# Linear attention with a routed expert layer on one core: the projection of the queries moved behind the first half of the products with the queries

## The chip, the core and the metric

The kernel runs on one core of a Trainium2 chip. The metric is the device time in microseconds (us) of one execution, the median of several runs. TensorE (PE in the profile; PEld is its loading of weights) does the matmuls, VectorE (DVE) and ScalarE (ACT) read their results out of PSUM, GpSimd (POOL) works in SBUF only, and SyncE (SP) issues most transfers.

## What is computed

The reference is a linear attention, whose rows then go through an expert layer that picks one expert per row. The change lies in the attention:

```python
def phi(x):
    proj = np.einsum('bhsd,df->bhsf', x, w_phi)
    proj = proj - np.max(np.abs(proj), axis=-1, keepdims=True)
    return np.concatenate([np.exp(proj), np.exp(-proj)], axis=-1)
q_p, k_p = (phi(q), phi(k))
kv = np.einsum('bhsf,bhsd->bhfd', k_p, v)
z = np.sum(k_p, axis=2)
num = np.einsum('bhsf,bhfd->bhsd', q_p, kv)
den = np.einsum('bhsf,bhf->bhs', q_p, z)[..., None] + 1e-06
return (num / den).astype(np.float32)
```

There are 8 batches, 8 heads, 576 rows of 64 numbers each, and 128 features; everything is float32. After it come 4608 rows of 512 for 8 experts (512 to 1024 and back).

## The kernel before

The attention is cut into 16 units (one batch, four heads) and each unit into two pairs of heads, so there are 32 steps for the keys and 32 for the queries. A software pipeline runs over iterations t = 0 to 37 (line 836). Each iteration works on a different stage of several steps at once: the keys' step t is transposed, that of t-1 projected, that of t-2 exponentiated and summed; the queries run two steps behind the keys (`lag`), and are projected at t-3, turned and exponentiated at t-4, and multiplied with the sums at t-5.

What an iteration does, in which order, is a string of letters in the table `CFG` (line 22): `order` has one string for even t and one for odd t, and `ends` has strings of its own for t = 34, 35 and 36. From t = 3 on the engines take the instructions in just that order (`man`: PE, DVE, ACT and POOL are scheduled by hand). The letters that matter here are these.

- `v` (`st_turn_more`, lines 441 to 465, even t only): transposes on PE into the PSUM tile `ps_V`, of the sums over keys (`kvs`) and of the queries' last rows (`ut`). ACT empties the tile by one copy to `kvt` (line 453) and two exponentials to `eqt` (line 462).
- `0`, `1`, `2` (`st_proj`, lines 386 to 409): projections on PE into a PSUM tile `ps_A` of two banks, `1` of a key step, `2` of a query step, `0` of the last rows (odd t only). There are two such tiles (`nb`, A: 2). DVE reads each twice (lines 405 and 406) and writes `u`.
- `a`, `b`, `c`, `d`: these two DVE instructions for `0` (a), `1` (b) and `2` (d); `c` holds the reciprocals and the transposes of the inputs.
- `K`: the two exponentials of a key step on ACT (line 420).
- `Q` (`st_turn_q`, lines 430 to 439): sixteen transposes of the queries' `u` on PE, into the same PSUM tag `ps_V`, of which there is one buffer (line 423). `e` and `E` are the two exponentials that ACT makes of them (line 437).
- `u` and `w` (`st_use_q`, lines 532 to 562): the first and the second half of the products of the queries with the sums, into `ps_O`, each emptied by ACT (line 549).
- `x` and `z` (`st_use_k`, lines 469 to 490): the sums over keys of the first and the second head, into `ps_K` (line 476).
- `l` (`st_logits`) and `y` (`st_use_qt`): small products behind them. `B` takes a bank of `ps_K`. `L`, `P`, `R`, `r` run what was put off: the routing of finished batches.

The loop that reads the strings is short:

```python
for c in CFG["ends"].get(t, CFG["order"][t % 2]):
    ...
    elif c == "2":
        x = pair("q", t - F - 1)
        if x:
            mx["2"] = st_proj([x[0]], x[1])
    ...
    elif c in "uw":
        if uq:
            st_use_q(*uq, int(c == "w"))
```

Of the kernel before, what the change touches and what calls it, by code (L numbers as in the profile page):

```python
# [18 lines left out]

P = 128  # L20
SLOT = 256
CFG = {'late': 1, 'sp': 1, 'gp': (6, 8, 11, 14, 16, 19, 21), 'rows': 9.0, 'tab': (2, 2, 3, 4, 5, 6, 7, 8, 9, 10, 11, 12, 15, 19, 31), 'ql': 0, 'cp': 0, 'seq': ('E', 'E', 'E', 'C', 'C', 'SC', 'C', 'DS', 'C', 'D'), 'post': (4, 8, 6), 'post2': (3, 5, 5), 'pk': (0, 2, 4), 'man': (3, 38), 'eng': ('PE', 'DVE', 'Activation', 'Pool'), 'nb': {'K': 1, 'O': 1, 'A': 2, 'P': 3, 'U': 2}, 'apools': (('ld', 2), ('hl', 4), ('up', 5), ('zp', 2), ('ep', 7), ('kvp', 5), ('ac', 1), ('xp', 3)), 'mpools': (('wseta', 1), ('mx', 1), ('mo', 2), ('wsetb', 1), ('wsetc', 1), ('rawq', 1)), 'lag': (2, 2, 3, 0), 'order': ('LPv12KQebRcdBuExzwlr', 'LP01aKQ2ebRcdBuExwzyr'), 'vl': 0, 'at': 1, 'eb': (2, 2), 'ub': 4, 'stage': (2, 2, 4, 4), 'stage2': (1, 2, 3, 3), 'dve': ('0', '1', 'ntkq', '2', 'n2', 'tkq', 'n2t'), 'pd': 1, 'vq': 0, 'qq': 1, 'xb': 4, 'whole': 'k', 'vb': 1, 'af': 1, 'wg': 2, 'q0': 1, 'out6': 2, 'ends': {34: '2dcvQeuEFBwlLRPr', 35: 'QcueERwyLXPr', 36: 'cuwRyLPr'}}


@with_exitstack
def kernel(
# [51 lines left out]
    edge.tile([P, 56], F32, name="edge")  # L78
    for nm, bufs in CFG["apools"]:
        c, side = (lctx, "right") if nm in ("ld", "hl") else (actx, "left")  # L80
        pools[nm] = c.enter_context(tc.tile_pool(name=nm, bufs=bufs, side=side))
    ac = pools["ac"]
    NB = CFG["nb"]

# [200 lines left out]
    with actx:  # L285
# [44 lines left out]
        def st_load(u, eng=nc.sync, more=None):  # L330
            whole = u.kind in CFG["whole"]
            w = D if whole else 32
            whole = whole and u.g >= CFG["wg"]
            u.raw = ld.tile([P, 2, 18, w], F32, tag="raw" + u.kind, name="raw", bufs=2)
            for pr in range(1 if whole else 2):
                for hd in range(2):
                    for dh in range(2):
                        r = slice((2 * hd + dh) * 32, (2 * hd + dh) * 32 + 32)
                        src = kv_in[u.kind][u.g][hd * 32:hd * 32 + 32]
                        if whole:  # L340

                            n = 18 * D - 32
                            nc.sync.dma_start(
                                out=u.raw[r].rearrange("p r t c -> p r (t c)")[:, :, 0:n],
                                in_=src[:, :, dh * 32:dh * 32 + n])
                        else:
                            (more if more and pr == 1 else eng).dma_start(
                                out=u.raw[r, pr, :, 0:32],
                                in_=src[:, pr].rearrange("p (t c) -> p t c", c=D)[:, :, dh * 32:dh * 32 + 32])

        def st_loadv(u):
            u.v0 = ld.tile([P, 4, 4 * D], F32, tag="v", name="v", bufs=CFG["vb"])
            u.vt = vts[u.g % len(vts)]
            for q4 in range(4):
                nc.sync.dma_start(
                    out=u.v0[q4 * 32:q4 * 32 + 32].rearrange("p h (t c) -> p h t c", c=D),
                    in_=vv[u.g][:, :, 4 * q4:4 * q4 + 4, :],
                )

            u.v1 = ld.tile([32, 4, 2 * D], F32, tag="v1", name="v1", bufs=CFG["vb"])  # L360
            nc.sync.dma_start(
                out=u.v1, in_=vv[u.g][:, :, 16:18, :].rearrange("p h t c -> p h (t c)"))
# [1089 lines left out]
```

## Time and profile before

| | us |
|---|---|
| median of 3 runs | 581.87 |
| lowest and highest | 579.68, 582.03 |
| the profiled execution's own time | 578.38 |
| its span, first to last instruction | 576.2 |
| the attention's pipeline, about t = 4 to t = 33 | 25.3 to 297 of the span |
| PE busy in that stretch | 250.22 of 271.70 |

A row of the timeline gives the start, the time from the first start to the last end of a run of like instructions, engine, line, what is written and read, the count, and in brackets the idle time ahead of it with what ended it. The records of one projection are 16, of `Q` 16, of `u` or `w` 32. Matmuls are pipelined, so how long a block holds up PE is read from its start to the next block's start, not from its duration.

### The profile page before, as it was taken

To read this page: it belongs to the slowest core of one execution; us is meant where nothing else is said; L and a number is where in the kernel's file an instruction comes from. 1 tells how busy PE (TensorE), PEld (TensorE's weight loads), DVE (VectorE), ACT (ScalarE), POOL (GpSimd) and SP (SyncE) were. 2 spreads that over 40 slices of the span, in tenths; PEclk is the share of its full clock that TensorE was granted. 3 is DMA by queue.
4 is the path that set the end of the run, shared out by engine and by line. 5 is a ranking of instruction groups with operands and counts; after the bars stand their busy time and mean duration, and the time that the engine had idled before them with its cause. 6 is when DMAs were issued, how large, how long until landed. Compare 5 with 4: busy or idle time off the path is not lost. (4 is left out here: it accounts for less than half of the span.)

```text
span 576.2 us, 20682 instructions
## 1 busy us (share of the span) xinstructions
PE 522.2 (91%) x8606; PEld 485.4 (84%) x8606; DVE 447.4 (78%) x790; ACT 341.9 (59%) x606; POOL 282.7 (49%) x520
## 2 busy tenths in 40 slices
PE   2888999998999898998989999799999989999993
PEld 2788999888998888998988898699889878988892
DVE  3887788988778887797966897778879898868840
ACT  1457676677666776677665443745676757646620
POOL 4213335635547354564546256683749571558011
PEclk9989999999999999999999999899999999999998
DMA  7878878788987989875367895679577986867400
GB/s 147 176 166 163 168 160 211 194 170 174 243 205 194 195 174 224 201 183 122 130 211 270 251 335 179 180 247 335 167 254 241 325 289 233 276 205 250 171 20 32
DMA packets 151233, 116.25 MB, mean 202 GB/s; under 512 B 91875, under 2 KB 126819, under 8 KB 150114
## 3 DMA queue, kind: packets, MB, share of 16 engines
q1 hardware_dynamic: 140704, 104.51, 66.7%
q0 software_dynamic: 3200, 9.45, 4.6%
q10 hardware_dynamic: 7234, 0.95, 1.0%
q8 instruction: 69, 1.13, 0.8%
q14 instruction: 26, 0.21, 0.1%
HBM read 91.66 MB, written 24.02 MB: 201 GB/s over the span
## 5 line engine op out<-in xcount | busy, mean ns | idle before, releaser
L217 POOL TENSOR_TENSOR w<-wraw_c,w 128x256 fp32r<-128x256 f32 x84 | 81.1, 994 | 54.2 <-ACT w L212 38.4
L405 DVE TENSOR_REDUCE m<-ps_A 128x8 f32<-128x1024 f32 x64 | 77.0, 1203 | 35.7 <-PE ps_A L395 35.7
L217 DVE TENSOR_TENSOR w<-wraw_c,w 128x1024 fp32r<-128x1024 f32 x71 | 94.0, 1340 | 12.8 <-ACT w L212 12.5
L212 ACT ACTIVATE w<-wraw_c 128x1024 fp32r<-128x1024 f32 x92 | 93.8, 1050 | 7.4 <-DMA wraw_c<-in_moe_w_dram 7.4
L476 PE MATMUL ps_K<-vm,ek 128*64 128x65 f32 x2048 | 79.9, 224 | 5.4 <-issue 3.0
L406 DVE TENSOR_TENSOR u<-ps_A,m 128x1024 f32<-128x1024 f32 x64 | 78.3, 1224 | 3.9
L545 PE MATMUL ps_O<-kva,eq 128*64 128x74 f32 x1984 | 76.8, 229 | 4.6 <-issue 4.0
L395 PE MATMUL ps_A<-wsrc,xT 64*128 64x128 f32 x1024 | 73.1, 289 | 7.2 <-DVE u L406 4.5
L476 PEld LDWEIGHTS ps_K<-vm,ek 128*64 128x64 f32 x2048 | 73.0, 140 | 5.5 <-issue 4.7
L545 PEld LDWEIGHTS ps_O<-kva,eq 128*64 128x64 f32 x1984 | 68.8, 136 | 8.2 <-issue 4.6
L395 PEld LDWEIGHTS ps_A<-wsrc,xT 64*128 64x128 f32 x1024 | 65.8, 199 | 10.2 <-DVE u L406 4.8
L437 ACT ACTIVATE eq<-ps_V 128x1024 f32<-128x1024 f32 x64 | 65.7, 1030 | 9.6 <-PE ps_V L428 9.6
L420 ACT ACTIVATE ek<-u 128x1024 f32<-128x1024 f32 x64 | 64.1, 1057 | 2.3 <-DVE u L406 2.3
L1110 PE MATMUL ps_O<-w,hh 128*128 128x512 f32 x160 | 63.7, 398 | 0.0
L1029 POOL DMA_INDIRECT out_dram<-o,si x22 | 28.8, 1307 | 59.5 <-DVE si L1025 46.0
L549 ACT ACTIVATE os<-ps_O 128x296 f32<-128x296 f32 x62 | 26.1, 420 | 48.4 <-PE ps_O L545 46.4
L1115 PE MATMUL ps_O<-w,hlo 128*128 128x512 f32 x120 | 47.2, 394 | 0.0
L1114 PE MATMUL ps_O<-w,hh 128*128 128x512 f32 x120 | 47.0, 391 | 0.0
L524 POOL TENSOR_TENSOR xm<-os,rec 128x512 f32<-128x512 f32 x32 | 33.4, 1045 | 24.9 <-DVE rec L523 21.5
L384 DVE STREAM_TRANSPOSE xT<-raw 128x512 f32<-128x512 f32 x64 | 40.5, 669 | 1.2 <-DMA raw<-in_k_dram 1.2
L476 PE MATMUL ps_K<-vt,ekt 128*64 128x65 f32 x512 | 37.7, 224 | 0.0
L1110 PEld LDWEIGHTS ps_O<-w,hh 128*128 128x128 f32 x160 | 30.1, 188 | 6.1
(283 smaller groups left out, 1084.9 us busy)
## 6 DMA issues: line engine op xcount, KB each, us to landing
wraw_c<-in_moe_w_dram SPq DMA_DIRECT2D x96, 512.0 KB, 5.3
raw<-in_k_dram SPq DMA_DIRECT2D x56, 280.0 KB, 5.3
raw<-in_q_dram SPq DMA_DIRECT2D x120, 72.0 KB, 4.6
xrows<-xm SPq DMA_DIRECT2D x8, 1028.0 KB, 5.8
v<-in_v_dram SPq DMA_DIRECT2D x64, 128.0 KB, 3.4
out_dram<-xm SPq DMA_DIRECT2D x32, 256.0 KB, 4.8
xrows<-xt SPq DMA_DIRECT2D x4, 257.0 KB, 6.0
v<-in_v_dram SPq DMA_DIRECT2D x16, 64.0 KB, 3.1
```

The costliest lines, as they stand in the source:

```text
L212: nc.scalar.activation(out=hi, in_=raw, func=AF.Copy)
L217: eng.tensor_tensor(out=lo[:, r], in0=raw[:, r], in1=hi[:, r].bitcast(F32), op=ALU.subtract)
L395: nc.tensor.matmul(p[:, hd, j * NF:(j + 1) * NF], xT[r], wsrc[r], start=True, stop=True)
L405: lambda: nc.vector.tensor_reduce(out=m, in_=pv, axis=AX.X, op=ALU.max, apply_absolute_value=True),
L406: lambda: nc.vector.tensor_tensor(out=uu, in0=pv, in1=m.rearrange("p h (j o) -> p h j o", o=1).broadcast_to([P, 2, n, NF]), op=ALU.subtract),
L420: nc.scalar.activation(out=o, in_=uu, func=AF.Exp, scale=(1.0, -1.0)[a])
L437: return [lambda a=a: nc.scalar.activation(out=e[:, a].rearrange("p s g c -> p s (g c)"), in_=t, func=AF.Exp, scale=(1.0, -1.0)[a]) for a ...
L476: nc.tensor.matmul(o[s * 64:s * 64 + 64, hd, half, :], e[:, half, s * 64:s * 64 + 64], x, start=(g == 0), stop=(g == 4))
L545: q_last[0] = nc.tensor.matmul(ov[s * 64:s * 64 + 64, 2 * j + hd, :], e[:, half, s, 4 * hd + 2 * th + j], kva[:, half, 2 * pr + hd, :], st ...
L1110: nc.tensor.matmul(y[sub], hh[:, t], wh[:, fi, :], start=first, stop=False)
L1114: nc.tensor.matmul(y[sub], hh[:, t], wl[:, fi, :], start=False, stop=False)
L1115: nc.tensor.matmul(y[sub], hlo[:, t], wh[:, fi, :], start=False, stop=last)
```

## The change

Two strings of `order` change, one for even and one for odd t:

```diff
-'order': ('LPv12KQebRcdBuExzwlr', 'LP01aKQ2ebRcdBuExwzyr')
+'order': ('LPv1KQeub2RcBdExzwlr', 'LP01aKQeu2bRcBdExwzyr')
```

On even t the queries' projection `2` goes from its place behind that of the keys, `1`, to one behind the products `u`; on odd t it goes from behind `Q` to behind `u`. To make that so, `u` is moved ahead of the DVE's chains `b`, `c`, `d`. The strings for t = 34 to 36 stay.

PE, an even iteration (t = 6). Before: `kvs` and `ut` are the transposes `v`, `xT_931` belongs to the keys and `xT_932` to the queries, `u_984` or `u_1004` is read by `Q`, `ps_O` is `u`, and `ps_K` is `x`.

```order
L428 MATMUL ps_V_1104<-ident_101,kvs_894 128x64 x8
L428 MATMUL ps_V_1104<-ident_101,ut_939 128x64 x4
L395 MATMUL ps_A_1122<-wsrc_114,xT_931 128x128 x8
L395 MATMUL ps_A_1133<-wsrc_114,xT_932 128x128 x8
L428 MATMUL ps_V_1150<-ident_101,u_984 128x64 x16
L545 MATMUL ps_O_1182<-kva_565,eq_957 64x74 x16
L476 MATMUL ps_K_1180<-vm1_110,ek_1147 64x65 x8
```

The same place now:

```order
L428 MATMUL ps_V_1104<-ident_101,kvs_894 128x64 x8
L428 MATMUL ps_V_1104<-ident_101,ut_939 128x64 x4
L395 MATMUL ps_A_1122<-wsrc_114,xT_931 128x128 x8
L428 MATMUL ps_V_1139<-ident_101,u_1004 128x64 x16
L545 MATMUL ps_O_1159<-kva_565,eq_957 64x74 x16
L395 MATMUL ps_A_1179<-wsrc_114,xT_932 128x128 x8
L476 MATMUL ps_K_1197<-vm1_110,ek_1136 64x65 x8
```

Between the transposes into `ps_V` of `v` and those of `Q`, which reuse the one buffer, there stands one projection, where two stood; the other now stands between two blocks of products.

PE, an odd iteration (t = 7), before: `xTt` is `0`, `xT_1086` the keys' projection `1`, `xT_1093` the queries' `2`.

```order
L395 MATMUL ps_A_1282<-wsrc_114,xTt_1094 128x128 x2
L395 MATMUL ps_A_1289<-wsrc_114,xT_1086 128x128 x8
L428 MATMUL ps_V_1305<-ident_101,u_1143 128x64 x16
L395 MATMUL ps_A_1323<-wsrc_114,xT_1093 128x128 x8
L545 MATMUL ps_O_1346<-kva_892,eq_1151 64x74 x16
L476 MATMUL ps_K_1344<-vm1_110,ek_1302 64x65 x8
```

And now:

```order
L395 MATMUL ps_A_1282<-wsrc_114,xTt_1094 128x128 x2
L395 MATMUL ps_A_1289<-wsrc_114,xT_1086 128x128 x8
L428 MATMUL ps_V_1305<-ident_101,u_1189 128x64 x16
L545 MATMUL ps_O_1325<-kva_892,eq_1140 64x74 x16
L395 MATMUL ps_A_1343<-wsrc_114,xT_1093 128x128 x8
L476 MATMUL ps_K_1361<-vm1_110,ek_1302 64x65 x8
```

Here `2` and `u` have changed places. DVE, POOL and SP keep their order throughout. On ACT the emptying of `u` (line 549) moves ahead of two small instructions of the routing (lines 647 and 660) where an iteration has one.

More of the change, by code (lines that the diff above doesn't have):

```diff
@@ L21 @@
 SLOT = 256
-CFG = {'late': 1, 'sp': 1, 'gp': (6, 8, 11, 14, 16, 19, 21), 'rows': 9.0, 'tab': (2, 2, 3, 4, 5, 6, 7, 8, 9, 10, 11, 12, 15, 19, 31), 'ql': 0, 'cp': 0, 'seq': ('E', 'E', 'E', 'C', 'C', 'SC', 'C', 'DS', 'C', 'D'), 'post': (4, 8, 6), 'post2': (3, 5, 5), 'pk': (0, 2, 4), 'man': (3, 38), 'eng': ('PE', 'DVE', 'Activation', 'Pool'), 'nb': {'K': 1, 'O': 1, 'A': 2, 'P': 3, 'U': 2}, 'apools': (('ld', 2), ('hl', 4), ('up', 5), ('zp', 2), ('ep', 7), ('kvp', 5), ('ac', 1), ('xp', 3)), 'mpools': (('wseta', 1), ('mx', 1), ('mo', 2), ('wsetb', 1), ('wsetc', 1), ('rawq', 1)), 'lag': (2, 2, 3, 0), 'order': ('LPv12KQebRcdBuExzwlr', 'LP01aKQ2ebRcdBuExwzyr'), 'vl': 0, 'at': 1, 'eb': (2, 2), 'ub': 4, 'stage': (2, 2, 4, 4), 'stage2': (1, 2, 3, 3), 'dve': ('0', '1', 'ntkq', '2', 'n2', 'tkq', 'n2t'), 'pd': 1, 'vq': 0, 'qq': 1, 'xb': 4, 'whole': 'k', 'vb': 1, 'af': 1, 'wg': 2, 'q0': 1, 'out6': 2, 'ends': {34: '2dcvQeuEFBwlLRPr', 35: 'QcueERwyLXPr', 36: 'cuwRyLPr'}}
+CFG = {'late': 1, 'sp': 1, 'gp': (6, 8, 11, 14, 16, 19, 21), 'rows': 9.0, 'tab': (2, 2, 3, 4, 5, 6, 7, 8, 9, 10, 11, 12, 15, 19, 31), 'ql': 0, 'cp': 0, 'seq': ('E', 'E', 'E', 'C', 'C', 'SC', 'C', 'DS', 'C', 'D'), 'post': (4, 8, 6), 'post2': (3, 5, 5), 'pk': (0, 2, 4), 'man': (3, 38), 'eng': ('PE', 'DVE', 'Activation', 'Pool'), 'nb': {'K': 1, 'O': 1, 'A': 2, 'P': 3, 'U': 2}, 'apools': (('ld', 2), ('hl', 4), ('up', 5), ('zp', 2), ('ep', 7), ('kvp', 5), ('ac', 1), ('xp', 3)), 'mpools': (('wseta', 1), ('mx', 1), ('mo', 2), ('wsetb', 1), ('wsetc', 1), ('rawq', 1)), 'lag': (2, 2, 3, 0), 'order': ('LPv1KQeub2RcBdExzwlr', 'LP01aKQeu2bRcBdExwzyr'), 'vl': 0, 'at': 1, 'eb': (2, 2), 'ub': 4, 'stage': (2, 2, 4, 4), 'stage2': (1, 2, 3, 3), 'dve': ('0', '1', 'ntkq', '2', 'n2', 'tkq', 'n2t'), 'pd': 1, 'vq': 0, 'qq': 1, 'xb': 4, 'whole': 'k', 'vb': 1, 'af': 1, 'wg': 2, 'q0': 1, 'out6': 2, 'ends': {34: '2dcvQeuEFBwlLRPr', 35: 'QcueERwyLXPr', 36: 'cuwRyLPr'}}
 @with_exitstack
```

## The prediction

> **What bounds the kernel now.** The page comes first: which engine is full, and for how long.
>
> ```profile
> span 576.2 us, 20682 instructions
> ...
> PE 522.2 (91%) x8606; PEld 485.4 (84%) x8606; DVE 447.4 (78%) x790; ACT 341.9 (59%) x606; POOL 282.7 (49%) x520
> ```
>
> PE leads over the whole span. The change touches only the attention's pipeline, so the second view is the table of stretches for it, whose columns are the length of the stretch and each engine's busy time in it.
>
> ```profile
> 25.30:297.00 271.70, 250.22 (x6543) 240.71 (x6541) 224.47 (x393) 183.81 (x333) 127.23 (x296) 0.99 0.78 180
> ```
>
> PE is busy for 250.22 of 271.70 us there, at a granted clock of 0.99; DVE follows with 224.47. So an instruction's worth of time added to PE is lost, unless PE would have idled for it. Where PE idles now is in the waits of PE in this same stretch (engine and line, what it waited for, us in total, times, longest).
>
> ```profile
> PE ps_A L395 <- DVE u L406: 4.5, 5, 1.3
> PE ps_O L545 <- issue: 4.0, 3, 1.8
> PE ps_K L476 <- issue: 3.0, 4, 1.1
> ...
> PE ps_A L395 <- DVE ut L406: 1.1, 5, 0.2
> ```
>
> Two of these waits belong to projections: PE waits for DVE to hand back a `ps_A` tile, five times for 0.9 us in the mean, at `1` of an odd iteration, and five times shortly at `2` of an odd iteration. The rows with "issue" are seven idle stretches that nothing in the profile ends. These rows are what may hide a new delay.
>
> **The part on even iterations: `Q` loses its cover.** The timeline of PE in an even iteration (t = 18) shows the order in which the one `ps_V` buffer is used twice.
>
> ```profile
> 150.74 0.47 PE L428 MATMUL ps_V<-ident,kvs 64*128 64x64 f32 x8
> 151.04 0.29 PE L428 MATMUL ps_V<-ident,ut 64*128 64x64 f32 x4
> 151.16 2.01 PE L395 MATMUL ps_A<-wsrc,xT 64*128 64x128 f32 x32
> 153.00 0.67 PE L428 MATMUL ps_V<-ident,u 64*128 64x64 f32 x16
> 153.60 1.25 PE L545 MATMUL ps_O<-kva,eq 128*64 128x74 f32 x32
> 154.68 0.64 PE L476 MATMUL ps_K<-vm,ek 128*64 128x65 f32 x16
> ```
>
> The 32 records at 151.16 are `1` and `2`; behind them `Q` starts at 153.00 without a wait. ACT in the same iteration:
>
> ```profile
> 151.86 0.66 ACT L462 ACTIVATE eqt<-ps_V 128x256 f32<-128x256 f32 x2
> ...
> 153.00 2.01 ACT L420 ACTIVATE ek<-u 128x1024 f32<-128x1024 f32 x2
> 154.90 1.03 ACT L437 ACTIVATE eq<-ps_V 128x1024 f32<-128x1024 f32 x1
> ```
>
> `Q` may not write `ps_V` before `eqt` is read out, at 151.86 + 0.66 = 152.52, which is 1.78 us behind the start of `v`. There is a place in the trace where nothing stands between: t = 34, whose own string has `v` and `Q` side by side.
>
> ```profile
> 297.37 0.41 PE L428 MATMUL ps_V<-ident,kvs 64*128 64x64 f32 x8
> ...
> 299.14 0.58 PEld L428 LDWEIGHTS ps_V<-ident,u 64*128 64x128 f32 x16 [1.38 <-ACT eqt L462]
> ```
>
> There `Q` starts 1.77 us behind `v` and has waited for `eqt`. With `1` alone between them, PE would be ready for `Q` one projection after 151.16. How long a projection holds PE ahead of `Q` is in the next odd iteration (t = 19):
>
> ```profile
> 160.12 1.06 PE L395 MATMUL ps_A<-wsrc,xT 64*128 64x128 f32 x16
> 161.02 0.66 PE L428 MATMUL ps_V<-ident,u 64*128 64x64 f32 x16
> 161.90 1.16 PE L395 MATMUL ps_A<-wsrc,xT 64*128 64x128 f32 x16 [0.22 <-DVE ut L406]
> 163.00 1.19 PE L545 MATMUL ps_O<-kva,eq 128*64 128x74 f32 x30
> ```
>
> It is 161.02 - 160.12 = 0.90, so PE is ready at 152.06, and waits until 150.74 + 1.77 = 152.51: a new stall of 0.45 us in each even iteration, of which there are fifteen (t = 4 to 32).
>
> **The part on both kinds: two more changes of shape.** The rows also say how the weights lie: `64*128` for `v`, `0`, `1`, `2` and `Q`, `128*64` for `u`, `w`, `x`, `z` and `l`. Before, an iteration has all of the first shape together; now `2` stands between `u` and `x`, and PE goes to the second shape, back, and there again. Blocks that meet at such a border are further apart. From an odd iteration (t = 17):
>
> ```profile
> 140.62 0.72 PE L395 MATMUL ps_A<-wsrc,xTt 64*128 64x128 f32 x8
> 142.30 1.16 PE L395 MATMUL ps_A<-wsrc,xT 64*128 64x128 f32 x16 [0.96 <-DVE u L406]
> 143.29 0.66 PE L428 MATMUL ps_V<-ident,u 64*128 64x64 f32 x16
> 143.78 1.11 PE L395 MATMUL ps_A<-wsrc,xT 64*128 64x128 f32 x16
> 144.83 1.25 PE L545 MATMUL ps_O<-kva,eq 128*64 128x74 f32 x32
> ...
> 145.91 0.63 PE L476 MATMUL ps_K<-vm,ek 128*64 128x65 f32 x16
> ```
>
> A projection ahead of products takes 144.83 - 143.78 = 1.05, against the 0.90 ahead of `Q`. `Q` ahead of a projection takes 0.49, ahead of products (153.00 to 153.60) 0.60. For products ahead of a projection, which the pipeline does not have now, the nearest rows are the 32 records of `y` ahead of one (t = 33), and for a projection ahead of sums those of t = 3:
>
> ```profile
> 295.24 1.20 PE L589 MATMUL ps_O<-kva,eqt 128*64 128x74 f32 x32
> 296.37 0.83 PE L395 MATMUL ps_A<-wsrc,xT 64*128 64x128 f32 x10
> ```
>
> ```profile
> 21.75 1.16 PE L395 MATMUL ps_A<-wsrc,xT 64*128 64x128 f32 x16 [0.72 <-DVE ut L406]
> 22.84 0.69 PE L476 MATMUL ps_K<-vm,ek 128*64 128x65 f32 x16
> ```
>
> 1.13 and 1.09; for the latter I take 1.05, as ahead of products, since t = 3 lies in the start. Now the two iterations can be laid out. Even, from `v` to `x`: before 154.68 - 150.74 = 3.94. After: `Q` at 1.77, then 0.60, 1.13 and 1.05, so `x` at 4.55: 0.61 more, 0.45 of it the stall and 0.16 the borders. Odd, from `Q` to `x`: before 145.91 - 143.29 = 2.62; after 0.60 + 1.13 + 1.05 = 2.78: 0.16 more. Per pair 0.77, over fifteen pairs 11.55 us, if nothing hides it.
>
> **What hides it.** First, the five long waits of PE for `u` at `1` of an odd iteration. DVE's row there starts from `1` of the even iteration, which doesn't move, and the wait ends when DVE is done; a PE that comes 0.61 later waits 0.61 less. 5 x 0.61 = 3.05 (the waits have 0.9 each). Second, the wait at `2` of an odd iteration goes: at t = 19 it stands 0.88 behind `Q` (161.02 to 161.90), at t = 17 0.49, so 0.39 each, and behind `u` the tile is long free. 5 x 0.39 = 1.95; by the idle times of the row alone, 1.1. Left are 11.55 - 3.05 - 1.95 = 6.55. Third, the idle stretches with "issue". Six of the seven stand in an even iteration behind `Q`, the first and the last of the four at line 476 being
>
> ```profile
> 122.23 0.22 PE L476 MATMUL ps_K<-vm,ek 128*64 128x65 f32 x1 [1.06 <-issue]
> ...
> 248.33 0.57 PE L476 MATMUL ps_K<-vm,ek 128*64 128x65 f32 x13 [0.52 <-issue]
> ```
>
> and none of the six is ahead of a long wait. If what ends them comes at a time of its own, each swallows up to 0.61: 6 x 0.61 = 3.66, and 2.89 are left. The Trainium skill, "Runtime: NRT & Kernel Launch", section "Instruction fetch mechanics", says that crossing from one block of fetched instructions to the next is mostly hidden; by that there would be no such idle time, nothing to swallow, and 6.55 would be the sum. The trace disagrees: the two rows of waits hold 7.0 us. So the sum lies between 2.9 and 6.55. I take 4.1, nearer to the lower end, because short waits at `1` that end under the modelled tail of `0` are not in the row and cover some too.
>
> What else moves costs nothing. DVE takes the result of `2` later than PE gives it:
>
> ```profile
> 157.51 1.19 DVE L405 TENSOR_REDUCE m<-ps_A 128x8 f32<-128x1024 f32 x1
> ...
> 165.60 1.19 DVE L405 TENSOR_REDUCE m<-ps_A 128x8 f32<-128x1024 f32 x1
> ```
>
> Even, `2` starts at 150.74 + 3.50 = 154.24 and is done 1.16 later, at 155.4, DVE comes at 157.51: 2.1 to spare. Odd, it starts at 161.02 + 0.61 + 1.73 = 163.36 and is done at 164.5, DVE comes at 165.60: 1.1 to spare. ACT's first exponential of `Q` waits for `ek` until 154.90, while `Q` is done at about 153.2. On ACT the emptying of `u` goes ahead of two small instructions; at worst they shift by one such copy and nobody on PE waits for them. SP's queue is the same, so no transfer moves by order.
>
> **The sum.** On the profiled execution 578.38 + 4.1 = 582.5. That run is 3.5 below the median of 581.87, with no row that says why, so the change is put on the median: 586.0. About 0.5% (2.9 us) is what a measurement of this kernel can tell from no change: slower means above 584.8, faster below 579.0.
>
> **The rivals.**
>
> *Covered after all (not slower).* The distance between blocks of different shape could be a matter of the buffers they touch and not come twice; then only the stalls count: 15 x 0.45 = 6.75, less 5 x 0.45 for the long waits, 1.95 at the odd `2`, and 6 x 0.45 = 2.7 in the issue stretches: -0.15. Time 581.7. It decides if `2` behind `u` starts 1.03 and not 1.13 later and `x` 0.90 behind `2`. For it: the covers are large, and two of the border's four numbers are taken from other blocks. Against it: both border prices that the pipeline has (1.05 against 0.90, 0.60 against 0.49) point the same way.
>
> *Nothing hides it (much slower).* The issue stretches stay, the waits of DVE move along with PE, since DVE's own inputs come from PE: 581.87 + 11.55 = 593.4. The Trainium skill, "Perfetto Trace Analysis", section "Optimization Strategy", says that the same gap repeating on the engine that should be saturated can mean that PSUM lacks room for the next tile; a gap ahead of `Q` would be just that, and by this rule it is a loss in each iteration. Against it: in the five pairs with a long wait DVE starts from `1`, ahead of the stall.
>
> *The stall feeds the issue (faster).* If the seven stretches come from PE's instructions arriving late, a PE that waits 0.45 us in each even iteration may let them arrive, and the seven go: -7.0. With the stalls alone left over (6.75 - 2.25 - 1.95 = 2.55) that makes -4.5, 577.4. It decides when at least 5.5 of the 7.0 us go and the borders are free. For it: 7.0 us are there to be had. Against it: a stretch of 1.8 is not cured by 0.45.
>
> **How the numbers follow.** The forecast, 2.9 to 6.55 more (584.8 to 588.4), has 0.60; covered after all 0.25; nothing hides it 0.06; faster 0.09. The forecast is slower but for its lowest edge, 0.51 of it, and so is the second rival: 0.57. No change is 0.25 and 0.09 of the forecast: 0.34. Faster 0.09. The range leaves out the second rival and most of the third, and allows for the spread of the runs of before at both ends: 580.0 to 590.0.
>
> **What would show it.** Right: in the waits of PE a row `ps_V` L428 <- ACT `eqt` of about fifteen times, 0.3 to 0.5 each; `Q` 1.77 behind `v` on even t; the row of `ut` gone; the row of `u` at `1` cut from 4.5 to about 1.5; `x` about 1.05 behind `2`. Wrong: if the `eqt` row is missing, if DVE waits for `ps_A` at `d`, or if the issue rows change by several us, since then the sum is not what decides. The experts' stage, from 297 on, should take as long as before.

## The result, and the profile after

The changed kernel takes 584.45 us (median of 22 runs, 580.64 to 588.53), the kernel before 581.27 (22 runs beside it, 577.97 to 583.61). The ratio is 1.0057, with a 95% interval of 1.004 to 1.0074: 3.3 us slower, between 2.3 and 4.3. The profiled execution took 584.05, its span is 581.9. The ratios here and below leave out runs that lasted over 1.5% longer than the fastest of their kernel, the medians don't, so the two can differ a little.

The first views of the changed kernel, as before: the page's span and engines, and the table of stretches for the same 25.3 to 297 us.

```profile
span 581.9 us, 20693 instructions
...
PE 532.2 (91%) x8606; PEld 488.0 (84%) x8606; DVE 446.7 (77%) x790; ACT 342.2 (59%) x606; POOL 281.7 (48%) x520
```

```profile
25.30:297.00 271.70, 254.89 (x6427) 239.02 (x6423) 223.20 (x393) 182.58 (x330) 124.87 (x291) 0.99 0.76 175
```

In the same 271.70 us PE records fewer matmuls, 6427 against 6543, and yet is busy for 4.7 us more: the pipeline runs slower while PE looks fuller (the rows of an iteration below show that part of a wait counts as busy). What PE waits for there (this answer covers 25.3 to 302, since the pipeline ends later):

```profile
PE ps_V L428 <- ACT eqt L462: 4.4, 15, 0.3
...
PE ps_O L545 <- issue: 1.6, 2, 1.1
...
PE ps_K L476 <- issue: 1.3, 4, 0.4
...
PE ps_A L395 <- DVE u L406: 0.9, 3, 0.5
...
PE ps_V L428 <- issue: 0.9, 1, 0.9
```

The new row is at the top, with fifteen entries. The row of `u` has gone from 4.5 to 0.9, that of `ut` is gone, and the idle time with "issue" is 3.8 instead of 7.7 us (the 4.0, the 3.0 and a 0.7 at line 395).

An even iteration (t = 10), PE and then ACT:

```profile
79.19 0.46 PE L428 MATMUL ps_V<-ident,kvs 64*128 64x64 f32 x8
...
79.61 1.11 PE L395 MATMUL ps_A<-wsrc,xT 64*128 64x128 f32 x16
81.02 0.71 PE L428 MATMUL ps_V<-ident,u 64*128 64x64 f32 x16 [0.30 <-ACT eqt L462]
81.66 1.25 PE L545 MATMUL ps_O<-kva,eq 128*64 128x74 f32 x32
82.84 1.16 PE L395 MATMUL ps_A<-wsrc,xT 64*128 64x128 f32 x16
83.93 0.28 PE L476 MATMUL ps_K<-vm,ek 128*64 128x65 f32 x2
```

```profile
80.31 0.66 ACT L462 ACTIVATE eqt<-ps_V 128x256 f32<-128x256 f32 x2
```

`Q` starts at 81.02, 0.05 behind the end of `eqt` at 80.97. PE was ready 0.90 behind 79.61, at 80.51, so by starts the stall is 0.51; the bracket shows only 0.30, since the modelled end of the last matmul lies over the beginning of the wait. `x` stands 4.74 behind `v`, where it was 3.94. The odd iteration behind it:

```profile
87.87 0.71 PE L395 MATMUL ps_A<-wsrc,xTt 64*128 64x128 f32 x8
88.54 1.16 PE L395 MATMUL ps_A<-wsrc,xT 64*128 64x128 f32 x16
89.51 0.69 PE L428 MATMUL ps_V<-ident,u 64*128 64x64 f32 x16
90.13 1.25 PE L545 MATMUL ps_O<-kva,eq 128*64 128x74 f32 x32
91.31 1.16 PE L395 MATMUL ps_A<-wsrc,xT 64*128 64x128 f32 x16
92.40 0.39 PE L476 MATMUL ps_K<-vm,ek 128*64 128x65 f32 x6
```

From `Q` to `x` it is 2.89 instead of 2.62. The long wait at `1` is gone. The same iteration (t = 11) of the kernel before:

```profile
87.69 0.72 PE L395 MATMUL ps_A<-wsrc,xTt 64*128 64x128 f32 x8
89.15 1.16 PE L395 MATMUL ps_A<-wsrc,xT 64*128 64x128 f32 x16 [0.74 <-DVE u L406]
```

From `0` to `1` it was 1.46 and is 88.54 - 87.87 = 0.67: 0.79 less, as much as `x` of the even iteration came later. DVE, which ends this wait, has not moved: it takes up `2` of t = 10 at 85.95, 6.76 behind `v`, and before at 86.65, 6.77 behind `v` (line 405).

### The profile page after: what moved, and what is told of

Same layout as the page of the kernel before. It is cut to its first block, busy times and chain, and to the rows that moved or that the text cites. A ratio compares the mean times of both kernels' runs of the same rounds, so it can differ in the third digit from the quotient of the medians.

```text
span 581.9 us, 20693 instructions
## 1 busy us (share of the span) xinstructions
PE 532.2 (91%) x8606; PEld 488.0 (84%) x8606; DVE 446.7 (77%) x790; ACT 342.2 (59%) x606; POOL 281.7 (48%) x520
## 3 DMA queue, kind: packets, MB, share of 16 engines
q8 instruction: 69, 1.13, 0.8%
## 5 line engine op out<-in xcount | busy, mean ns | idle before, releaser
L217 POOL TENSOR_TENSOR w<-wraw_c,w 128x256 fp32r<-128x256 f32 x84 | 79.9, 981 | 53.8 <-ACT w L212 37.8
L476 PE MATMUL ps_K<-vm,ek 128*64 128x65 f32 x2048 | 81.4, 224 | 2.8 <-ACT ek L420 2.1
L395 PE MATMUL ps_A<-wsrc,xT 64*128 64x128 f32 x1024 | 75.3, 288 | 2.0 <-DVE u L406 0.9
L524 POOL TENSOR_TENSOR xm<-os,rec 128x512 f32<-128x512 f32 x32 | 33.5, 1046 | 26.7 <-DVE rec L523 23.7
```

The source lines that it names most:

```text
L217: eng.tensor_tensor(out=lo[:, r], in0=raw[:, r], in1=hi[:, r].bitcast(F32), op=ALU.subtract)
L395: nc.tensor.matmul(p[:, hd, j * NF:(j + 1) * NF], xT[r], wsrc[r], start=True, stop=True)
L476: nc.tensor.matmul(o[s * 64:s * 64 + 64, hd, half, :], e[:, half, s * 64:s * 64 + 64], x, start=(g == 0), stop=(g == 4))
```

## The experiments

Theory: fifteen stalls for `eqt` and the added borders between weight shapes cost PE time, and part of it is hidden by idle time that PE had: the waits for `u` and `ut`, and the stretches with "issue". Rivals: the stall alone costs, or the borders alone, or nothing is hidden, or the issue stretches have nothing to do with it. Each ratio is to the kernel before, run beside it, with its 95% interval.

### One kind of iteration alone

```diff
-'order': ('LPv12KQebRcdBuExzwlr', 'LP01aKQ2ebRcdBuExwzyr')
+'order': ('LPv1KQeub2RcBdExzwlr', 'LP01aKQ2ebRcdBuExwzyr')
```

> The even string of the changed kernel, the odd string of before. Theory (a stall ahead of the turns plus two more borders between weight shapes, partly hidden by waits that were there): in each even iteration x stands 4.74 us behind v instead of 3.93 (0.46 stall, 0.35 borders), the wait of PE for eqt has about 15 entries, the five waits for ut at the odd projection stay (1.1 us), and of the gross 15 x 0.81 = 12.2 us about 1.2 to 2.6 are left: ratio 1.002 to 1.0045. Rival (all that is left comes from the odd iterations, the even ones are fully covered): ratio 1.000. Rival (nothing hides it): 12.2 us, ratio 1.021.

Measured: 1.0064 (1.0033 to 1.0095), 586.93 against 582.9. The row for `eqt` stands as in the changed kernel (4.4 us, 15 times), that for `ut` stays (0.9 us, 4 times). The even iterations alone cost as much as the whole change. Both rivals lie outside the interval; the ratio is above the expected 1.002 to 1.0045, though its interval reaches into it.

```diff
-'order': ('LPv12KQebRcdBuExzwlr', 'LP01aKQ2ebRcdBuExwzyr')
+'order': ('LPv12KQebRcdBuExzwlr', 'LP01aKQeu2bRcdBExwzyr')
```

> The odd string of the changed kernel, the even string of before. Theory: no wait for eqt; the row of waits for ut goes (5 x 0.39 us gained), each odd iteration pays 0.27 us for two more borders (4.05 us in all), so +1 to +2.1 us: ratio 1.002 to 1.004. Rival (the stall ahead of the turns is the whole cost, borders are free): 1.95 us faster, ratio 0.9965.

Measured: 1.000 (0.997 to 1.003). No wait for `eqt` but the old one at t = 34, none for `ut`, and the row of `u` rises from 4.5 to 5.8 us. The expected 1.002 to 1.004 lies at the upper end of the interval and beyond. By rows, 15 x 0.27 = 4.05 for the borders, less 1.95 for `ut`, plus 1.3 for `u`, less 0.8 for issue (6.9 instead of 7.7) would be a loss of 2.6; the interval allows 1.7, so some 0.9 is not placed. The 1.95 us of gain that free borders would have given (0.9965) are just outside the interval too.

### The stall and the borders apart

The first of these two kernels has `2` behind `Q` and ahead of `u` on even t: the same short cover for `Q`, but no added border.

```diff
-'order': ('LPv12KQebRcdBuExzwlr', 'LP01aKQ2ebRcdBuExwzyr')
+'order': ('LPv1KQ2ebRcdBuExzwlr', 'LP01aKQ2ebRcdBuExwzyr')
```

> Even iterations only: the queries' projection goes from behind that of the keys to behind the turns, ahead of the products, so that the turns stand behind one projection as in the changed kernel, but no border between weight shapes is added. Odd iterations as before. Theory: the wait for eqt with about 15 entries, 0.46 us each by the distance of starts, 6.9 us gross; the long waits at the odd projection hide 2.3, short ones 0.8, the unexplained idle stretches up to 2.7: +1.1 to +3.8 us, ratio 1.002 to 1.0065. Rival (the borders are the whole cost, the stall is hidden): ratio 1.000.

Measured: 1.0039 (1.0009 to 1.0069). PE at t = 10:

```profile
79.54 0.46 PE L428 MATMUL ps_V<-ident,kvs 64*128 64x64 f32 x8
...
79.97 1.11 PE L395 MATMUL ps_A<-wsrc,xT 64*128 64x128 f32 x16
81.37 0.71 PE L428 MATMUL ps_V<-ident,u 64*128 64x64 f32 x16 [0.30 <-ACT eqt L462]
81.92 1.11 PE L395 MATMUL ps_A<-wsrc,xT 64*128 64x128 f32 x16
82.96 1.25 PE L545 MATMUL ps_O<-kva,eq 128*64 128x74 f32 x32
84.04 0.34 PE L476 MATMUL ps_K<-vm,ek 128*64 128x65 f32 x6
```

The stall is the changed kernel's, and `x` stands 4.50 behind `v`, 0.56 more than before. So the stall costs time without any border, by an interval that clears 1 by 0.09%. The second kernel has the products between the two uses of `ps_V`, and `2` behind `Q`: as many borders as the change, no stall. It moves ACT too: the emptying of `u` goes ahead of both exponentials of `Q` (84.36 and 84.65 at t = 10), where before it stood between them.

```diff
-'order': ('LPv12KQebRcdBuExzwlr', 'LP01aKQ2ebRcdBuExwzyr')
+'order': ('LPv1KuQeb2RcBdExzwlr', 'LP01aKQ2ebRcdBuExwzyr')
```

> Even iterations only: keys' projection, first half of the products, turns, queries' projection, sums: as many borders between weight shapes as in the changed kernel, but the products stand between the two uses of the turning buffer. Odd iterations as before. Theory: no wait for eqt; x about 0.35 us later behind v, 15 x 0.35 = 5.25 us gross, of which the waits at the odd projection hide 2.5 and the unexplained stretches up to 2.1: +0.6 to +2.7 us, ratio 1.001 to 1.005. Rival (the stall is the whole cost): ratio 1.000.

Measured: 1.0028 (0.9997 to 1.006). PE at t = 10:

```profile
80.20 0.46 PE L428 MATMUL ps_V<-ident,kvs 64*128 64x64 f32 x8
...
80.62 1.11 PE L395 MATMUL ps_A<-wsrc,xT 64*128 64x128 f32 x16
81.66 1.25 PE L545 MATMUL ps_O<-kva,eq 128*64 128x74 f32 x32
82.84 0.72 PE L428 MATMUL ps_V<-ident,u 64*128 64x64 f32 x16
83.39 1.11 PE L395 MATMUL ps_A<-wsrc,xT 64*128 64x128 f32 x16
84.43 0.39 PE L476 MATMUL ps_K<-vm,ek 128*64 128x65 f32 x5
```

No wait in these rows (the whole pipeline has one for `eqt`, of 0.3), yet `x` stands 4.23 behind `v`, 0.29 more than before. The borders alone lengthen the iteration. That they also lengthen the run is not shown: the interval touches 1, and the medians, 583.27 and 582.9, differ by 0.06%. The sum of the two ratios, 0.67%, is near the 0.64% of the even string, but each is known to 0.3% only. The row of `u` is 4.6 (7 times) and seems to hide nothing. Yet at t = 11 `1` stands 1.18 behind `0` instead of 1.46, 0.28 less, about what `x` came later; what fills the row again is mainly t = 15, where 0.74 became 1.66. The kernel before has an issue stretch of 1.06 in the iteration ahead of it (122.23), which this one has not.

### What hides a loss, and what doesn't

The next two add work instead of idle time: the sixteen transposes of `Q` are made twice into the same place, first on even t, then on odd t (`== 1`, t from 5).

```diff
-        def st_turn_q(u, pr):
+        def st_turn_q(u, pr, times=1):
...
-            for c in range(8):
+            for c in range(8 * times):
+                c %= 8
...
-                    qx = st_turn_q(*tq)
+                    qx = st_turn_q(*tq, 2 if t % 2 == 0 and 4 <= t < 34 else 1)
```

> The kernel before, with the sixteen transposes of the turns (Q) made twice into the same place on even t from 4 to 32: about 0.58 us more of PE work in each of fifteen even iterations, behind the keys' projection, with no wait for eqt and no border between weight shapes; 8.7 us gross. Theory (what PE loses there is partly hidden): the five long waits at the odd projection hide 2.9, short ones there about 0.8, the unexplained idle stretches behind it up to 3.5; 1.5 to 5.0 us are left, ratio 1.0025 to 1.0085. Rival (nothing hides it, DVE's wait moves along with PE): 8.7 us, ratio 1.015.

Measured: 1.009 (1.006 to 1.0121), just above the expected 1.0025 to 1.0085. An even iteration and what PE waited for in all (the edit adds a line, so L546 is line 545 of the others):

```profile
80.75 0.46 PE L428 MATMUL ps_V<-ident,kvs 64*128 64x64 f32 x8
...
83.02 1.17 PE L428 MATMUL ps_V<-ident,u 64*128 64x64 f32 x32
84.11 1.25 PE L546 MATMUL ps_O<-kva,eq 128*64 128x74 f32 x32
85.19 0.28 PE L477 MATMUL ps_K<-vm,ek 128*64 128x65 f32 x2
```

```profile
PE ps_K L477 <- issue: 3.9, 4, 1.4
PE ps_O L546 <- issue: 2.8, 4, 1.3
PE ps_A L395 <- DVE u L406: 2.1, 5, 0.9
...
PE ps_A L395 <- issue: 1.2, 1, 1.2
```

`x` stands 4.44 behind `v`, 0.50 more than before, 7.5 us over fifteen iterations. The waits for `u` hid 4.5 - 2.1 = 2.4; the issue stretches hid nothing, they hold 8.1 us (with one of 0.2). 7.5 - 2.4 = 5.1, and 0.9% of 579.15 is 5.2, though the interval spans 3.5 to 7.0.

> The same on odd t from 5 to 33: the same 8.7 us of PE work, but behind the long waits and ahead of the queries' projection. Theory: only the waits for ut hide some of it, 5 x 0.39 = 1.95 us; with an unexplained stretch or two 5.5 to 6.8 us are left, ratio 1.0095 to 1.012, clearly more than on even t. Rival (idle time of PE hides it wherever it stands): as on even t. Rival (nothing hides it): ratio 1.015.

Measured: 1.0067 (1.0041 to 1.0092). The row of `u` is 4.1, that of `ut` is gone, issue 8.0. The same account, 7.5 - 0.4 - 1.95 = 5.2, is 1.3 more than 0.67% of 579.15, 3.9, and at the upper end of the interval. The expected 1.0095 to 1.012 was too high and the order of the two kernels is not what was expected; their intervals overlap, so these two times don't show that the place decides. In the waits it does: on even t the added work shortens the wait for `u`, on odd t that for `ut`.

The last of this group moves `Q` of even iterations right behind `v`, ahead of both projections; the order of no other engine changes.

```diff
-'order': ('LPv12KQebRcdBuExzwlr', 'LP01aKQ2ebRcdBuExwzyr')
+'order': ('LPvKQ12ebRcdBuExzwlr', 'LP01aKQ2ebRcdBuExwzyr')
```

> The kernel before, with the turns (Q) of even iterations ahead of both projections, right behind the transposes that use the same buffer (v); nothing else moves on any engine. The stall for eqt is then the whole 1.4 us, and it stands ahead of the keys' projection, from which DVE starts. By starts x comes about 1.5 us later behind v, 15 x 1.5 = 22.5 us gross. Theory (a loss behind the keys' projection is hidden by the waits for u at the next odd projection, one ahead of it is not, because DVE starts as much later): the row of waits for u stays or grows from 4.5 us, 22 to 27 us slower, ratio 1.038 to 1.046. Rival (those waits hide a loss wherever it stands): the row of u falls to under 1 us, 17 to 18 us slower, ratio about 1.030. If PE that idles lets its instructions catch up, the idle stretches with issue fall below 3 us; if they have nothing to do with it, 5 to 9 us as in the runs without a stall.

Measured: 1.0399 (1.0356 to 1.0443), 603.86 against 579.95. What PE waits for (25.3 to 320), and the iteration:

```profile
PE ps_V L428 <- ACT eqt L462: 18.7, 15, 1.2
PE ps_A L395 <- DVE u L406: 14.1, 13, 1.7
```

```profile
81.54 0.46 PE L428 MATMUL ps_V<-ident,kvs 64*128 64x64 f32 x8
...
83.37 0.71 PE L428 MATMUL ps_V<-ident,u 64*128 64x64 f32 x16 [1.25 <-ACT eqt L462]
83.92 2.00 PE L395 MATMUL ps_A<-wsrc,xT 64*128 64x128 f32 x32
85.85 1.25 PE L545 MATMUL ps_O<-kva,eq 128*64 128x74 f32 x32
86.93 0.64 PE L476 MATMUL ps_K<-vm,ek 128*64 128x65 f32 x16
...
92.77 0.49 PE L395 MATMUL ps_A<-wsrc,xT 64*128 64x128 f32 x4 [1.24 <-DVE u L406]
```

`x` stands 5.39 behind `v`, 1.45 more, 21.8 us in all; the waits for `u` grew by 9.6, from 5 to 13 of them, instead of shrinking; and the row with issue, 7.7 us before, is gone altogether. 21.8 + 9.6 - 7.7 = 23.7, and 3.99% of 579.95 is 23.1. Not all of it is the stall. `1`, from which DVE starts, stands 2.38 behind `v` instead of 0.42, so DVE starts 1.96 later and `x` only 1.45: the move of `Q` itself gives the four long waits of t = 11, 13, 17 and 21 some 0.5 each. The larger part of the growth is six new waits of 0.9 to 1.7 at t = 15, 19, 23, 25, 27 and 29, each behind one of the six even iterations in which the kernel before has an issue stretch. There a stretch had stood in the place of a wait for `u`: in a second profile of the kernel before, which lacks the stretch of t = 14, `1` of t = 15 stands 1.83 behind `0`, in the first 0.74. So a loss behind `1` eats into the waits for `u`, and one ahead of `1` does not, because DVE starts at least as much later.

### Is the issue time chance?

> The kernel before, a second look, for the idle stretches of PE with issue in the attention's pipeline: 7.7 us in the first profile of it, 5.4 to 9.2 us in six other kernels without a new stall. If these differ between kernels because of the stall: again 5 us or more here. If they are chance: anything from 3 to 9 us.

> The changed kernel, a second look, for the same stretches: 3.8 us in its first profile, 3.2 and 5.6 us in the two other kernels with the stall. If the stall lets PE's instructions arrive in time: again under 5 us. If the first was chance: anything from 3 to 9 us.

> The kernel with the stall alone on even iterations, a second look, for the same stretches: 5.6 us in its first profile. If the stall lets PE's instructions arrive in time: under 5 us; if chance: anything from 3 to 9 us.

Three second looks, one execution each, for the idle stretches with issue alone. All kernels, us (the 9.2 comes from an execution of 585.03 us, the longest of its twelve):

| PE idles more in even iterations | | no new idle time | |
|---|---|---|---|
| changed kernel, two looks | 3.8, 4.9 | before, two looks | 7.7, 5.9 |
| even string alone | 3.2 | odd string alone | 6.9 |
| stall alone, two looks | 5.6, 3.6 | borders alone | 5.4 |
| `Q` right behind `v` | 0 | turns twice, even and odd | 8.1, 8.0 |
| | | routing late, old and new odd string | 9.2, 6.4 |

But for one overlap (5.6 against 5.4) the two columns lie apart, and the kernel with by far the most idle time has none. So it is hardly chance: where PE idles for another reason, these stretches are shorter. The second looks alone, 5.9 and 4.9, differ by 1.0 only. Added work doesn't shrink the stretches (8.1), but it also adds instructions for PE, so it isn't a pure counterpart. Their place is not chance either. The kernel before, first and second look:

```profile
194.85 0.87 PE L545 MATMUL ps_O<-kva,eq 128*64 128x74 f32 x21 [1.53 <-issue]
```

```profile
194.51 0.87 PE L545 MATMUL ps_O<-kva,eq 128*64 128x74 f32 x21 [1.77 <-issue]
```

Both stand ahead of the last 21 records of the same block. So do those at 157.98 and 157.40 (last 30 records, 0.74 and 1.50 long) and at 211.21 and 210.90 (last 9, 0.73 and 0.77). The stretches at 122.23 and 221.76 have no counterpart in the second look. So the place goes mostly with the program, and the length changes from execution to execution.

### Two attempts at a faster kernel

The long waits for `u` lie in odd iterations before which DVE does routing work in its chain. The letter `R` goes behind `d`, first with the old odd string, then with the changed kernel's.

```diff
-'order': ('LPv12KQebRcdBuExzwlr', 'LP01aKQ2ebRcdBuExwzyr')
+'order': ('LPv12KQebcdRBuExzwlr', 'LP01aKQ2ebRcdBuExwzyr')
```

> Even string only: the put-off routing work (R) goes behind the DVE's chain for the queries' projection (d) instead of ahead of the chain c, so that DVE hands back the tile that the next odd iteration's keys' projection waits for by about 1.3 us earlier where a batch is routed. PE and ACT keep their order. Theory (the long waits of PE at the odd projection come from the routing on DVE): the row of waits for u falls from 4.5 us to under 1; but DVE then does the routing ahead of ut, so the queries' projection of that odd iteration waits for ut instead, about 1 us where it waits now 0; gain 0.5 to 1.5 us, ratio 0.9975 to 0.999. Rival (those waits come from elsewhere): the row stays, ratio 1.000.

Measured: 1.000 (0.9971 to 1.0028), so the expected gain (0.9975 to 0.999) is not shown. In the profile of its longest execution the row of `u` falls to 0.9, and that of `ut` rises to 4.6 us, 10 times, from 1.1: the wait has moved by one projection, as expected, and is no shorter.

```diff
-'order': ('LPv12KQebRcdBuExzwlr', 'LP01aKQ2ebRcdBuExwzyr')
+'order': ('LPv12KQebcdRBuExzwlr', 'LP01aKQeu2bRcdBExwzyr')
```

> The even string with the routing behind d, and the odd string of the changed kernel (queries' projection behind the products). Theory: the long waits for u go, and the wait for ut that would take their place is covered by the products, at the price of two borders (0.27 us) in each odd iteration, which by themselves measured no difference: 3 to 5 us faster than before, ratio 0.991 to 0.995. Rival (routing that comes later delays its own chain, or DVE is late elsewhere): ratio 1.000 or above.

Measured: 1.002 (0.9993 to 1.0048). The expected gain is not there. Its waits for `ut` are gone and `u` is down to one of 2.3 us, but PE now waits for POOL at `v`:

```profile
PE ps_V L428 <- POOL kvs L488: 3.7, 7, 0.9
```

against 2.0 us and three times in the changed kernel. With the borders of the odd string that uses up part of what was gained; the rest was not traced. No kernel here beats the one before.

## Why the prediction was right

- **The stall of `Q`.** Predicted 0.45 in each of fifteen even iterations; measured 15 entries, and 0.51 by starts at t = 10. That the stall alone costs is shown by the kernel with `2` behind `Q`. The row at t = 34, where the same two blocks stood side by side before, had given the distance (1.77; measured 81.02 - 79.19 = 1.83). At t = 4 the stall costs nothing: there are no products yet, and from `v` to the next `0` it is 8.25 before and 8.26 after. So fourteen even iterations count, not fifteen.
- **The borders.** Predicted 0.16 in either kind of iteration; measured 4.74 - 3.94 - 0.51 = 0.29 and 2.89 - 2.62 = 0.27. This term was mis-sized, nearly by half: `u` starts 0.64 behind `Q`, not 0.60, `2` 1.18 behind `u`, not 1.13, `x` 1.09 behind `2`, as at t = 3 and not 1.05, and the sum per pair is 0.80 + 0.27 = 1.07 instead of 0.77. The distances of blocks show it without any wait in the row (4.23 in the kernel with borders alone). The Trainium skill, "TensorEngine Tiling (Array Packing)", section "Key Properties", says that changing the tiling mode, and not just the tile, drains TensorE. The rows fit that and put the price of two more changes at about 0.3 us; whether it is a drain they don't show.
- **The long waits.** Predicted that they hide 3.05; their row fell by 3.6. The condition, that DVE starts ahead of the stall, holds at t = 10, where DVE takes up `2` 6.76 behind `v` as before, and the kernel with `Q` ahead of `1` shows the other case: DVE starts later, and nothing is hidden. This is also where the rival "nothing hides it" came out, with the Trainium skill's rule of the repeating gap ("Perfetto Trace Analysis", "Optimization Strategy"): the gap ahead of `Q` is there fifteen times and does stand for a buffer that is missing, but in some iterations it lies over a gap that was there before.
- **The wait for `ut`.** Predicted gone; it is gone, and the odd string alone is no slower.
- **The issue stretches.** This step had the wrong reason. Predicted that they swallow up to 3.66, as something that comes at a time of its own. They did lose 3.9 in the first profile (1.0 between the second looks), but most of them stand ahead of the same instruction in two executions, and where work was added instead of idle time they stayed as long. That leans to the rival "the stall feeds the issue", which is right in direction and too small to turn the sign: it needed 5.5 us and free borders. None of the six lies ahead of a long wait, as predicted, but the stretch can itself stand in the place of one, as at t = 14: the two covers aren't separate. The prediction also named a change of several us in these rows as a sign that its sum doesn't decide. That sign came, so the agreement of this term is luck. What ends these stretches the profile doesn't show. That the trace disagrees with the rule which the prediction cites there would hold only if they were waits for instructions, which no run shows.
- **The sum.** Gross 14 x 0.80 + 15 x 0.27 = 15.25 instead of 11.55; less 3.6, 1.95 and 3.9 leaves 5.8. The profiles give from the first `v` to the first matmul of the experts

```profile
25.32 0.34 PE L428 MATMUL ps_V<-ident,kvs 64*128 64x64 f32 x4
...
312.92 0.60 PE L1097 MATMUL ps_P<-x,wraw_c 128*128 128x256 f32 x2
```

before, and after

```profile
25.44 0.34 PE L428 MATMUL ps_V<-ident,kvs 64*128 64x64 f32 x4
...
317.74 0.81 PE L1097 MATMUL ps_P<-x,wraw_c 128*128 128x256 f32 x3
```

287.60 and 292.30, so 4.7. Part of the difference to 5.8 is the clock at t = 5 in the profile of before:

```profile
35.50:38.50 3.00, 2.91 (x34) 2.94 (x36) 2.07 (x3) 0.31 (x1) 2.12 (x5) 0.53 1.02 215
```

The granted clock is 0.53 in these 3 us, and 1.00 in the same 3 us of the changed kernel. From `1` to `u` it is 39.70 - 35.59 = 4.11 there, against 144.83 - 142.30 = 2.53 at t = 17: 1.6 us that the changed kernel did not lose here. 5.8 - 1.6 = 4.2 against 4.7, which is the account of this one pair of executions. The medians give 3.3, the forecast was 4.1. That the two are this near is partly luck: too cheap a border and too small a cover went against each other, and the forecast was a choice between 2.9 and 6.55. Single executions differ by more than the effect (the second looks took 576.74 and 586.73 us). The experts' stage is the same to 0.9 us (263.3 and 264.2).

## What to carry to other kernels

Before a step is moved, ask what it stands between: here the queries' projection covered the emptying of a single PSUM buffer, and it kept blocks of one weight shape together; neither service shows in a row of the profile. A loss on the full engine was hidden here only by idle time that comes later and whose end doesn't move with it; look for where the engine that ends that wait takes its start. Before two rows of idle time are counted as two covers, see whether one stands in the place of the other. Price a border between two kinds of matmuls by the distance of block starts, with several rows of the same pair, since no wait in a row shows it.

## What the runs showed of the hardware

A stall on TensorE reads shorter than it is: 0.30 us in the bracket where the starts give 0.51. Two more changes between weights of 64x128 and 128x64 cost 0.27 to 0.29 us an iteration with no wait shown. Idle stretches of PE without a cause in the profile, 5.4 to 9.2 us over the attention, fall to 3.2 to 5.6 where PE waits a further 0.5 us in every second iteration, and to none where it waits some 1.4 us there; 7.5 us of added work leave them at 8.1 and 8.0. In two executions of one kernel three of them stand ahead of the same record of the same block, 0.73 to 1.77 us long. The granted clock fell to 0.53 over 3 us in one execution (35.5 to 38.5), which cost 1.6 us.
